# Strided attention and a gated MLP on one core: early weight loads that wait for a tile, the pairs' last step in another order, one total later, and a tile of its own for each last half

## The chip, the cores and the metric

The kernel runs on one core of a Trainium2 chip. The metric is the device time of one execution in microseconds (us). Lower is better. Its engines are PE (matrix products), DVE (vector), ACT (activations), POOL and SP; SP and ACT also issue DMAs. SBUF holds the tiles, and PE writes into PSUM banks.

## What is computed

The reference, cut to what matters: attention over 8 batches, 8 heads, 576 positions and head size 64 with two sparse masks (the first four heads see the last 32 positions, the other four the positions with the same residue modulo 32), then RMS norm and a gated MLP on the 4608 tokens.

```python
mask_local = (rel >= 0) & (rel < 32)
mask_strided = (rel >= 0) & (pos[None, :] % 32 == pos[:, None] % 32)
scores = np.where(masks, q @ k.T / 8, -1e9)
x = (softmax(scores) @ v)                    # 4608 tokens x 512
xn = x / sqrt(mean(x * x) + 1e-6) * rms_g
g, val = xn @ w_gate, xn @ w_val             # 512 x 1536 each
out = (g * sigmoid(g) * val) @ w_out         # 1536 x 512
```

## The kernel before

Work is cut into 32 attention units (one batch, two heads; 576 positions) and 9 chunks of 512 tokens. `unit_s` computes a unit's scores and the softmax, `unit_o` the product with v. Four units run ahead of everything ("the prologue"); the others are strewn between the matrix products by the tables `WIN`, `SAT`, `OAT`, `PSAT`, `POAT`. The MLP splits each fp32 operand in a high and a low part and multiplies three times (`gemm1`, `slot_o`). Chunks 0 to 2 run plainly, twelve steps u of 128 hidden columns each. Chunks 3 to 8 run as three pairs (`pair_of_chunks`) with seven products, named "1" to "7", instead of eight.

Weights: `convert_weights` takes 1 MB of one weight as 64-bit words from DRAM into a tile `raw_` of four slots and turns it into fp32 high and low parts: ACT scales (L840) and builds exponents (L842), DVE does two bit operations (L844, L846), ACT or DVE copies the high part (L496/L498), DVE subtracts (L849). There are 18 such weights: 12 `gv` (gate and value columns of one u) and 6 `o` (output rows of two u). In order of conversion they are numbered here from 1: gv0, gv1, o0, gv2, gv3, o1, gv4 are weights 1 to 7.

SBUF for this is 94 slots of 128x512 words. `group(n)` gives n slots; the table `PLACE` names the slot of every request, and whoever gets a slot waits until its last owner is done with it. `Plan.order` is a list scheduler inside the kernel program: it writes the order of every engine's instructions from estimated costs, and engines then run their queues in that order, each instruction behind the waits of those ahead of it. From chunk 1 on the matrix products and all else on PE keep the order in which the program names them (`plan.serial`). In the gaps that the scheduler estimates on PE in the first 50 us, `fill` puts matmuls on zeros.

In a pair, each u of a quad adds its products into banks p, q and r: "1", "6", "7" and "4" all add into p. After "6" ACT copies p; after "7" DVE adds p to a tile (L1131); after "3" DVE adds to r (L1105) and multiplies (L1127). Between "7" and "4" of one u stands "1" of the next u, which goes into other banks; the last u, 11, has no next one. Then `oproduct` (L1220) multiplies by the output weights, with `attention(13)`, `attention(14)` and so on as marks between the products; between 14 and 15 no product stands. `rms(c)` sums squares on PE into the bank `pair` ("the total", L762), which the units use too, and ACT takes the logarithm from it (L766).

Of the kernel before, what the change touches and what calls it, by code (L numbers as in the profile page):

```python
# [75 lines left out]
RATP = {3: (13, 15), 5: (13, 15)}  # L76
PLACE = list(bytes.fromhex(
    "0004080c100e14181c1e50515253542022555657585924265a5b5c5d282c2d2e292a2f3034383c404414000408502b480c1052494a201c243057554c"
    "4b4e38404d4f5c14040c3c5a2b5020242e2c525c573808140c4d2b5020305a522e4849381420384d3c5c4a2e5a574b2b4d0c4e4f505c572e505c5354"
    "58595d5748495120565b2d564a4b4c285b56512f2e2d4c382856514e385b56512f5b4c3c565148382f4d4c56514c4e0c384a4b480c2f4c5651562f4e"  # L80
    "4f205156480c2f51564a4b2f2d2f4848280c515648282d505c535458595d575156553c525a525a5156525a554a4b482855522c3851562d2c55515648"
    "182d48283451562d4a4b515648204b2d441851564b4647515648004548280c0d0e0f4b47515648102021444f22234b1c1d483c1e1f40414243515647"
    "00015502030405060728292a2b5038393a3b5c53545859242526275d570e0f0c0d58454448104b47555b59085a52090a4f4e0b204b5521222e2f2334"
    "353233363037313c143d153e163f175b1c1d4d5d4c474849575a104b11551252135845594432183119301a3d1b4f25244e264b553e3f275a0e4c0f4d"
    "0c3d0d084b0944453f5d0a4e0b57203021312223441c5a5d1d583459354b3657371430155a4e444c164d1759104b115a121358184c30594b19271a26"
    "1b250e240f0c580d26251c081d09200a210b22235835090a4c4d34263627374d145815164d274d261710111213515618191a1b0e0f0c0d501c1d1e1f"
    "5c5453404142430100020908031751560405060728292a2b0e353438393a26503b1650202123220f36375c5453414014151011121349503b0d0c1819"
    "1a1b0e515616174243081c1d1e1f555d09470100020352575814050406073a28292a2b0f5c5438395342434140353436375b1c153b5a20214b23222f"
    "51560e0d0c16171011131218191a1b4e4f080a0b09303331325d55381d52243d57582e271e1f2547533945464b4a443c14503f3e5b15014849002f02"
    "2c2d035a3b2e0a3d09270b052404255d065507482042214352354134403c57582c363d37531c5a1d2f38392e304445314733463248505b1e1f251424"  # L90
    "5515423b5a4b534a40090a410b3d2e44485201460047025a035320213d052425044806520742504138395a35243d3452374736463b421c1d481e245a"
    "3332301f311424155209320a0b304b48244a4750462052214801004652020305040607145438393b3a5c5135343736561c1d1e1f2322081617282931"
    "304647472a2b0f0e0d0c091514540a0b101113120203504f474e18191a1b5c514b4a56010005040607504f584738393b3a1054222321203736343531"
    "1c1d1f1e34083045090a0b355d054e28292a2b5c115b5316171415510c0d0e0f5613124f501c1054044b4a030200240148434906071a1b1918553736"
    "525a3b3a39382223202159572d2e2c2f1d4e0c053e3d5d5c4231563432403554413f4f5027250d04433c584c4d30330f260e2445594420461e471f3d"
    "211c3e0a42570932083f0b31103013122b1d2a280029034002415c5d4b4a54585642503105324e4404464f59472d27262f242c252e56343e350c3f0d"
    "54310e400f414d2a4c2b2021325c295458445047003f105613124702272503241f2a1e291c3f1d593208274409410a400b474e294f052a0427244a47"
    "4b325c27355834502a2759535b2d2c2e2f514d4c0a0d0c0e0f555a520809202100020301060710124732131153594a515b37361f1e1d1c0d22234849"
    "504b5c04055a5255161715140c4e4f3435002a405951531b1a19184a5b0f0e3a3b393801030241570b0a09084d4c2f2e2d2c37365c504b555a525820"
    "2159530023225107065b055d56"))  # L100
# [247 lines left out]
def attn_moe(ctx: ExitStack, tc: tile.TileContext, qT: bass.AP, kT: bass.AP, vl: bass.AP,  # L348
# [178 lines left out]
    def load(i):  # L527
# [39 lines left out]
    tio = {}  # L567

    def unit_s(i):
# [887 lines left out]
```

## Time and profile before

| what | value |
|---|---|
| median of 3 runs | 949.81 us (948.96 to 949.81) |
| profiled execution | 950.59 us, its span 948.8 us |
| busy PE / DVE / ACT / POOL | 926.6 / 715.6 / 463.2 / 153.9 us |
| DMA | 214.94 MB, mean 227 GB/s |

The span runs from the first to the last instruction. 1.79 us of the profiled execution lie around its span, and it is 0.78 us above the median. Busy time of PE includes slow matmuls and matmuls on zeros, so stretches have to be read one by one.

### The profile page before, as it was taken

The numbers are of one execution on the slowest core, as the hardware profiler recorded it, in microseconds if no ns is written. First come the engines' busy times: TensorE is split into PE (matmuls) and PEld (weight loads), VectorE is DVE, ScalarE is ACT, GpSimd is POOL, SyncE is SP. The second block draws the span as 40 slices with busy tenths as digits, with TensorE's granted clock in tenths as the row PEclk, the third lists the DMA queues.
The fourth block names the chain that finished last, engine by engine and source line by source line (L and its number), as shares of the span: only waits on it lengthen the run. The fifth ranks groups of instructions, "written<-read, shape, count | busy, mean of one in ns | idle before, by whom it ended". The sixth has DMA issues, their size and how long they took to land.

```text
span 948.8 us, 18579 instructions
## 1 busy us (share of the span) xinstructions
PE 926.6 (98%) x7364; PEld 752.5 (79%) x7364; DVE 715.6 (75%) x1097; ACT 463.2 (49%) x723; POOL 153.9 (16%) x125
## 2 busy tenths in 40 slices
PE   6989999999999999999999999999999999999998
PEld 5678877888888888888887788888878877888786
DVE  5899989988599979775568899554698983345783
ACT  6797665343334247454446582443464733233440
POOL 1021302123043420210015031000140210000100
PEclk9899999999999999999999999999999999999999
DMA  9955756978668567997464638984434499741542
GB/s 356 407 219 184 260 200 238 346 263 303 220 211 288 167 217 267 304 393 232 144 200 159 198 127 293 392 253 140 145 100 157 161 365 338 194 149 59 165 154 90
DMA packets 122487, 214.94 MB, mean 227 GB/s; under 512 B 10784, under 2 KB 66336, under 8 KB 119328
## 3 DMA queue, kind: packets, MB, share of 16 engines
q1 hardware_dynamic: 121680, 213.16, 66.0%
q8 instruction: 58, 0.95, 0.4%
q10 hardware_dynamic: 720, 0.59, 0.2%
q14 instruction: 29, 0.24, 0.1%
HBM read 169.67 MB, written 44.04 MB: 225 GB/s over the span
## 4 chain that ended last, share of the span: by engine, by line
PE 87%; DMA 5%; DVE 4%; ACT 1%; issue 1%; SPq 0%; ACTq 0%; DVEq 0%
PE a L1094 16%; PE v L1094 10%; PE g L1094 10%; PE g L931 9%; PE a L983 9%; PE v L931 9%; PE a L1220 8%; PE g L1220 5%; PE v L1220 5%; PE pair L675 4%; PE pair L599 3%; DMA bl<-in_wgv_dram 2%; DMA bl<-gvd 1%; DVE bl L849 1%; DMA bl<-in_wo_dram 1%
## 5 line engine op out<-in xcount | busy, mean ns | idle before, releaser
L496 ACT CAST bl<-bl 128x512 fp32r<-128x512 f32 (+1 forms) x170 | 109.0, 665 | 116.2 <-DVE bl L1051 19.6
L1094 PE MATMUL a<-bl,bl 128*128 128x512 f32 x642 | 159.0, 393 | 0.0
L504 DVE TENSOR_TENSOR bl<-bl,bl 128x512 fp32r<-128x512 f32 x192 | 132.6, 716 | 10.4 <-PE a L1220 4.0
L1094 PEld LDWEIGHTS a<-bl,bl 128*128 128x128 f32 x642 | 119.0, 188 | 25.3
L1094 PE MATMUL v<-bl,bl 128*128 128x512 f32 x431 | 109.9, 390 | 2.9 <-DVE bl L1131 2.4
L931 PE MATMUL g<-bl,bl 128*128 128x512 f32 x408 | 107.1, 398 | 3.5 <-DVE bl L849 3.0
L1094 PE MATMUL g<-bl,bl 128*128 128x512 f32 x428 | 109.2, 390 | 0.7 <-ACT bl L1110 0.7
L931 PE MATMUL v<-bl,bl 128*128 128x512 f32 x420 | 109.4, 397 | 0.1
L983 PE MATMUL a<-bl,bl 128*128 128x512 f32 x432 | 107.0, 389 | 1.1 <-DVE bl L849 1.1
L1094 PEld LDWEIGHTS v<-bl,bl 128*128 128x128 f32 x431 | 80.6, 188 | 21.2 <-DVE bl L1131 3.7
L983 PEld LDWEIGHTS a<-bl,bl 128*128 128x128 f32 x432 | 81.0, 188 | 18.3 <-DVE bl L849 1.5
L1051 DVE TENSOR_TENSOR bl<-bl,bl 128x512 f32<-128x512 f32 x104 | 72.2, 708 | 30.5 <-ACT bl L1110 28.7
L1094 PEld LDWEIGHTS g<-bl,bl 128*128 128x128 f32 x428 | 80.0, 188 | 17.9 <-ACT bl L1110 1.1
L1105 DVE TENSOR_TENSOR a<-a,bl 128x512 f32<-128x512 f32 x72 | 49.8, 695 | 58.9 <-PE a L1094 46.5
L931 PEld LDWEIGHTS g<-bl,bl 128*128 128x128 f32 x408 | 75.4, 189 | 21.8 <-DVE bl L849 4.3
L931 PEld LDWEIGHTS v<-bl,bl 128*128 128x128 f32 x420 | 78.2, 189 | 17.9 <-DVE bl L966 0.8
L504 POOL TENSOR_TENSOR bl<-bl,bl 128x512 fp32r<-128x512 f32 x28 | 41.0, 1467 | 254.9 <-PE g L1094 89.7
L1220 PE MATMUL a<-bl,bl 128*128 128x512 f32 x306 | 72.1, 390 | 0.0
L1220 PEld LDWEIGHTS a<-bl,bl 128*128 128x128 f32 x306 | 57.3, 188 | 12.4 <-DVE bl L504 0.5
L498 DVE CAST bl<-bl 128x512 fp32r<-128x512 f32 (+1 forms) x86 | 48.1, 564 | 15.7 <-PE a L983 3.5
L1051 POOL TENSOR_TENSOR bl<-bl,bl 128x512 f32<-128x512 f32 x20 | 27.2, 1367 | 148.6 <-DVE bl L504 52.2
L1220 PE MATMUL g<-bl,bl 128*128 128x512 f32 x214 | 50.9, 390 | 0.0
(164 smaller groups left out, 1276.8 us busy)
## 6 DMA issues: line engine op xcount, KB each, us to landing
bl<-gvd SPq DMA_DIRECT2D x252, 256.0 KB, 4.9
gvd<-bl SPq DMA_DIRECT2D x72, 256.0 KB, 4.0
bl<-to SPq DMA_DIRECT2D x72, 256.0 KB, 4.1
xq<-in_qT_dram SPq DMA_DIRECT2D x28, 576.0 KB, 5.4
bl<-wos SPq DMA_DIRECT2D x54, 256.0 KB, 3.3
bl<-in_wgv_dram SPq DMA_DIRECT2D x12, 1024.0 KB, 9.6
bl<-wos SPq DMA_DIRECT2D x12, 1024.0 KB, 6.7
vt<-in_vl_dram SPq DMA_DIRECT2D x28, 320.0 KB, 4.0
```

The source lines that it names most:

```text
L496: nc.scalar.copy(out=o, in_=i)
L498: nc.vector.tensor_copy(out=o, in_=i)
L504: elementwise(CH, lambda e: both(e).tensor_tensor(out=lo.new(F32R), in0=src(), in1=hi.f32(), op=ALU.subtract), reads + [hi.key], [lo.key])
L599: nc.tensor.matmul(out=pr[at // CH][64 * s:64 * s + 64, at % CH:at % CH + KW], lhsT=tq()[:, 2 * q0:2 * q0 + 64], rhs=tk_()[:, q0:q0 + KW], ...
L675: nc.tensor.matmul(out=pr[s][64 * h:64 * h + 64, 32 * lo:32 * hi], lhsT=va()[r:r + 32, D * kb:D * kb + D], rhs=pT[r:r + 32, 64 * kb - 32 * ...
L849: elementwise(2 * CH, lambda e: both(e).tensor_tensor(out=wide(q[2:], F32R), in0=cell(1).bitcast(F32), in1=wide(q[:2]), op=ALU.subtract), ...
L931: nc.tensor.matmul(out=out_, lhsT=w.t[:, sl], rhs=x.t, start=(kc == 0 and i == 0), stop=(kc == KC - 1 and i == 2))
L983: nc.tensor.matmul(out=acc[t], lhsT=x.t[:, sl], rhs=w.t, start=(u == 0 and i == 0), stop=(u == NU - 1 and i == 2))
L1051: elementwise(CH, lambda e: both(e).tensor_tensor(out=o.new() if fresh else o.t, in0=a.t, in1=b.t, op=how), [a.key, b.key], [o.key])
L1094: nc.tensor.matmul(out=banks[bk], lhsT=w, rhs=xs[k][y].t, start=start and k == 0 and i == 0, stop=stop and k == 1 and i == 2, skip_group_c ...
L1105: op("DVE", dve(CH), 0, lambda: nc.vector.tensor_tensor(out=banks[bk], in0=banks[bk], in1=t.t, op=ALU.add), reads=[t.key], writes=[bk])
L1220: nc.tensor.matmul(out=banks[bks[j]], lhsT=v, rhs=xs[k][y].t, start=start and k == 0 and i == 0, stop=stop and k == KT - 1 and i == 2, ski ...
```

## The change

The early loads: the raw tile of weights 2 and 3 is now the four slots in which units 2 and 3 of the prologue keep their probabilities and their transpose (`GATE`), and weights 4 to 7 take the raw tile of the weight three before (`REUSE`). So each waits for that tile's last reader. Loads of units 4 and 5 are put in the scheduler at 30 and 36 us (`REL`), and the second mask constant is loaded ahead of unit 2's queries. The last u of a pair runs its products as 5, 6, 2, 7, 3, 4 instead of 5, 6, 2, 3, 7, 4. In pair 3 the total of chunk 5 stands at mark 14 instead of 13. Each half of the last output tiles has a slot of its own, so the DVE copy no longer follows the ACT copy. Fills have 512 columns instead of 192, and one is put per 400 ns of estimated gap instead of 200. `PLACE` is a new table throughout. The diff (the table of slots and the two other loads of a unit, which get the same `rel`, are cut):

```diff
-FILLS = 200.0
+FILLS = 400.0
-FILLN = 192
-LOADS = ("q0", "c2", "c0", "q1", "q2", "v0", "c1", "q3", "v1", "w", "v2", "v3")
+FILLN = 512
+LOADS = ('q0','c2','c0','q1','c1','q2','v0','q3','v1','w','v2','v3')
-RATP = {3: (13, 15), 5: (13, 15)}
+RATP = {3:(14,15),5:(13,15)}
 PLACE = list(bytes.fromhex(
...
+LASTQ = '56273'
+TAILS = True
+REUSE = 3
+GATE = True
+REL = {4:30e3,5:36e3}
...
-    def group(n, r=False):
+    def group(n, r=False, want=None):
...
+        if want is not None and kind[home[want]] in (None, r) and all(want + k in freed for k in range(n)):
+            best = 0, want
         i = PLACE[m] if PLACE and m < len(PLACE) else best[1]
...
-    still = sbt([P, 256], "still", BF16)
+    still = sbt([P, max(256, FILLN)], "still", BF16)
...
-        op("SP", 430, 0, lambda: nc.sync.dma_start(out=tq(), in_=qT[b, p]), writes=keys_[:1], bytes_=P * S * 8, follow="SP" if pro else None)
+        op("SP", 430, 0, lambda: nc.sync.dma_start(out=tq(), in_=qT[b, p]), writes=keys_[:1], bytes_=P * S * 8, rel=REL.get(i, 0.0), follow="SP" if pro else None)
...
         if 1 < i < NPRO:
-            z, y = take2(), take2()
+            zz = group(4) if GATE else take2() + take2()
+            z, y = zz[:2], zz[2:]
+            gates.append(zz[0].i)
...
+    raws = []
+
     def convert_weights(what, u):
-        raw_, q = group(4), group(4, True)
+        raw_ = group(4, False, raws[-REUSE] if REUSE and REUSE <= len(raws) < 7 else gates[len(raws) - 1] if GATE and len(raws) in (1, 2) else None)
+        raws.append(raw_[0].i)
+        q = group(4, True)
...
-            order += [(u, m) for m in ("56237" if u > 1 else "")] + [(u + 1, "1")] * (u + 1 < NU) + [(u, "4")]
+            order += [(u, m) for m in (LASTQ if u == NU - 1 else "56237" if u > 1 else "")] + [(u + 1, "1")] * (u + 1 < NU) + [(u, "4")]
...
-                for m in "56237":
+                for m in LASTQ if u == NU - 1 else "56237":
...
         for j in range(2):
-            dst = take()
             for n, (e, q) in enumerate((("ACT", nc.scalar), ("DVE", nc.sync))):
+                if n == 0 or TAILS:
+                    dst = take()
                 sl = slice(256 * n, 256 * n + 256)
-
-                def half(e=e, sl=sl, dst=dst, j=j, n=n):
-                    copy_to(e, (dst.new() if n == 0 else dst.t)[:, sl], banks[P2[j]][:, sl])
-                op(e, 310, 0, half, reads=[P2[j]] + [dst.key] * n, writes=[("oh", c, j, n)] + [dst.key] * (1 - n))
+                lead = n == 0 or TAILS
+
+                def half(e=e, sl=sl, dst=dst, j=j, lead=lead):
+                    copy_to(e, (dst.new() if lead else dst.t)[:, sl], banks[P2[j]][:, sl])
+                op(e, 310, 0, half, reads=[P2[j]] + [dst.key] * (not lead), writes=[("oh", c, j, n)] + [dst.key] * lead)
...
-            give(dst)
+                if n or TAILS:
+                    give(dst)
```

## Rows read from the trace of the kernel before

**Rows 1.** Busy time of each engine (the page's first part), and in stretches: busy us (and instructions) of PE, PE's weight loads, DVE, ACT and POOL, then the granted PE clock, the DMA share and GB/s.

```profile
PE 926.6 (98%) x7364; PEld 752.5 (79%) x7364; DVE 715.6 (75%) x1097; ACT 463.2 (49%) x723; POOL 153.9 (16%) x125
...
23.00:26.00 3.00, 3.00 (x82) 2.73 (x82) 3.00 (x4) 2.74 (x3) 0.61 (x1) 0.50 1.04 416
26.00:29.00 3.00, 3.00 (x4) 0.83 (x3) 3.00 (x4) 3.00 (x8) 1.49 (x1) 0.50 1.03 407
...
50.00:54.00 4.00, 4.00 (x13) 3.09 (x12) 3.97 (x5) 4.00 (x4) 1.74 (x2) 0.58 0.97 403
...
60.00:70.00 10.00, 9.94 (x43) 7.88 (x44) 10.00 (x10) 8.12 (x9) 1.73 (x1) 1.00 0.57 210
...
160.00:270.00 110.00, 110.00 (x1104) 89.66 (x1103) 88.09 (x142) 41.31 (x50) 21.39 (x16) 1.00 0.77 263
```

**Rows 2.** PE's timeline: start, busy us, line, operation, count, and in brackets the idle time before it with what ended it.

```profile
1.43 3.54 PE L518 MATMUL v<-still 128*128 128x192 bf16 x21 [1.43 <-POOL still L514]
6.51 0.31 PE L594 MATMUL g<-cb,identb 128*128 128x320 bf16 x1 [1.54 <-DMA identb<-in_consts_dram]
...
23.11 2.41 PE L675 MATMUL a<-bl,bl 32*64 32x64 f32 x80
...
39.38 0.84 PE L931 MATMUL a<-bl,bl 128*128 128x512 f32 x3
...
46.47 0.39 PE L931 MATMUL g<-bl,bl 128*128 128x512 f32 x1
49.53 0.90 PE L931 MATMUL g<-bl,bl 128*128 128x512 f32 x2 [2.67 <-DVE bl L849]
...
54.44 0.84 PE L931 MATMUL v<-bl,bl 128*128 128x512 f32 x3
...
59.90 2.14 PE L931 MATMUL g<-bl,bl 128*128 128x512 f32 x8 [0.30 <-DVE bl L849]
```

**Rows 3.** The same view of ACT and DVE, before PE's wait of rows 2.

```profile
44.51 1.17 ACT L840 ACTIVATE bl<-bl 128x1024 f32<-128x1024 f32 x1 [3.87 <-DMA bl<-in_wgv_dram]
45.69 1.28 ACT L950 ACT_TABLE_LOAD   x1
46.99 0.63 ACT L950 ACTIVATE bl<-bl 128x512 f32<-128x512 f32 x1
...
36.32 1.21 DVE L849 TENSOR_TENSOR bl<-bl,bl 128x1024 fp32r<-128x1024 f32 x1
...
44.49 0.68 DVE L498 CAST bl<-bl 128x1024 fp32r<-128x1024 f32 x1
47.65 0.69 DVE L966 TENSOR_TENSOR bl<-bl,v 128x512 f32<-128x512 f32 x1 [2.48 <-ACT bl L950]
48.26 1.22 DVE L849 TENSOR_TENSOR bl<-bl,bl 128x1024 fp32r<-128x1024 f32 x1
```

**Rows 4.** Loads of weights: SP's issues (start, us, line), then the issues of 0 to 60 us and of 60 to 150 us by kind (count, KB of one, median us from issue to landing).

```profile
25.88 2.92 SPq L835 DMA_DIRECT2D bl<-in_wgv_dram  x2
31.08 0.37 SPq L835 DMA_DIRECT2D bl<-in_wo_dram  x1
31.61 0.37 SPq L835 DMA_DIRECT2D bl<-in_wgv_dram  x1
...
bl<-in_wgv_dram SPq DMA_DIRECT2D x8, 1024.0 KB, 11.0
...
bl<-in_wgv_dram SPq DMA_DIRECT2D x5, 1024.0 KB, 5.3
```

**Rows 5.** PE's waits from 120 to 160 us: who, on what, us in total, times, longest.

```profile
PE a L983 <- DVE bl L849: 1.1, 1, 1.1
PE pair L762 <- DVE bl L504: 0.4, 1, 0.4
PE g L931 <- DVE bl L504: 0.3, 1, 0.3
```

**Rows 6.** The end of the third pair's last u on the chain of work that ended last (start, us, what), and the waits of PE for L1131 in the whole span.

```profile
884.16 1.37 PE v L1094 x6
...
885.62 0.70 DVE bl L1131
...
886.37 1.66 PE v L1094 x6
888.02 4.08 PE g L1220 x18
...
PE v L1094 <- DVE bl L1131: 2.4, 3, 0.9
```

**Rows 7.** The first total in pair 3: the timeline of PE and ACT around it.

```profile
541.73 1.17 ACT L496 COPY bl<-pair 128x64 f32<-128x64 f32 x4 [3.52 <-PE pair L675]
542.96 0.73 PE L762 MATMUL pair<-bl,onesr 128*128 128x512 f32 x2 [1.29 <-ACT bl L496]
543.52 2.69 PE L1220 MATMUL a<-bl,bl 128*128 128x512 f32 x11
545.43 0.69 ACT L766 ACTIVATE bl<-pair,few 128x512 f32<-128x512 f32 x1
```

**Rows 8.** The last copies, from the timeline.

```profile
945.18 0.37 ACT L496 COPY bl<-v 128x256 f32<-128x256 f32 x1 [3.71 <-PE v L1220]
...
945.58 0.42 DVE L498 COPY bl<-v 128x256 f32<-128x256 f32 x1 [3.66 <-ACT bl L496]
```

More of the change, by code (lines that the diff above doesn't have):

```diff
@@ L75 @@
 RAT = {0: (10,), 1: (9,), 2: (8, 9)}
-RATP = {3: (13, 15), 5: (13, 15)}
+RATP = {3:(14,15),5:(13,15)}
 PLACE = list(bytes.fromhex(
[L78 to L100, printed above, removed]
@@ L101 @@
-HALFQ = (3,)
+    "0004080c100e14181c1e5051525354205556575859245a5b5c5d282c2d2e292a2f203024341438203c2440482b4a1444494b4c0004080c4e4f504d52"
+    "101c57555c202414005a2b5208342e2c4e4a4b10201440485557080c495a4e5c4c101408102e002b4d524e55574a2e085c4b2b5748554a5257534c4d"
+    "5458595d4940504851565c4b2e285b595d552d504810285c4b2e105156595b555d005c4b4810515d2e56592f4808105c4b48085b512e56595b2f2e40"
+    "5c4b48085b56595c4b5b505b5c4828084b5648285c594a5257505354584b562c005a5c48494b565a5c2c28294e102c5a4c182a2b4d564c4b484e102c"
@@ new lines @@
+    "4e304049284d2c4e292a38103a3b4d3c4b2b4f4e4d484938304d08444b28292a0a0b1011380412133a4f00012e02031c302b242526272a48491e2928"
+    "1f4445464718191a1b343536374b0405060720212223000108090a0b594a12134d4c38403a4f2e551011525d5750515354585b2d0c0d5c5a0e0f301c"
+    "1d311e321f2f334f21551438153916173a222e5b525d232d59514a53401c41424d434c5502380357001f011e3c3d4f3e50542e583f51083a09530a2d"
+    "0b1257131f505838104f115921534a3a0c0d4c0e4d1f0f51223823573059313253334f141516401741384257434f2102510316533857004d014c4a51"
@@ new lines @@
+    "3c4c3d3e513f16170816094d0a510b4d121351100c0d0e0f1116220c230f214a51300c0f0c16313233404142430809020300013c3d3e3f4b202b2a29"
+    "2848492524262744161845474631323334353736040506070002030a1a1b0b3001080912131011404142434a4b2223211916204918063c3d3e3f3120"
+    "48492b2a2928321b3324252627045d5b0544454746280732343537365430535a595157000102030a0b0809063343424041315c12131118104a0d4b29"
+    "2b2a222321203d3c3e3f48495d5b4c4d55501f1d1c1e0128563252071b2d393a58044f0f05550d1806243b2f25262e2c275c14170203441516454e47"
@@ new lines @@
+    "191b464f3139330f500d34353a37153b362d112c122e132f2832180a19560f52390b15085809420143551f401e413a1d2e1c4e5c4f075806042c052d"
+    "150219031850423141242540262e184219192719332d322c112e28444f454e4047554619125c131934352d372c5c362c01550a2d0b500809551f2d4e"
+    "4f2d2c1e2d1d2c1c55312c02035528070611043305320724252d26550527121344454746015430531d5a59511f1e570034353736100a0b0809295507"
+    "045d5b5b2b2a284a4b27111c543130532223212048493d3c5b3e3f4c4d12131d0a5a5159265702030100335207324544474624251f1e22550b103d04"
@@ new lines @@
+    "273c1c0809545b18533534373631304a4b29282a2b3d572311105c581d0a21205a5051593e3f121348494c4d2255060b333b32262725241f1e020301"
+    "00454447465b562d2f2e2c5d141617153c54531c3a39040d1d084341090a19185a2a1b1a31304e4f5051404259292852064a054b3b383507340e370f"
+    "360c212039550d4322412f3a120413525d3e543f53492e482c4e3c4f4d3b4c5a0d1c07051d190a18081b091a502a39143a04150e160f175351415931"
+    "54304807290d28555d1b223a4a4b39204e4f2153121813192f482c2e5435555a344e370f360e3c1b3e3f390a0d501c531d552a540818094d194c5951"
@@ L102 @@
+    "5d4e3139300d22285529540f1415161720214a4b2b131257235c0a2f2e2c590b5853353437361011543e0e193f3c3d33321c1d5b562d1f1e5d2a2627"
+    "252457020300012b454447464d4c5c1312375909394e0858531415161729284a4b0a0b20212223540d0e5d3635343130565b10112f2e2c2d33323e3f"
+    "3c3d5c571c1d1f1e5a5152555919064305"))
+HALFQ = (3,)
+LASTQ = '56273'
[3 more added lines that the diff above has]
+REL = {4:30e3,5:36e3}
 LEAD = 12
@@ L537, in load @@
             op("Pool", 100, 0, lambda: nc.gpsimd.memset(tk_()[:, 0:PAD], 0.0), writes=keys_[2:])
-        op("SP", 430, 0, lambda: nc.sync.dma_start(out=tq(), in_=qT[b, p]), writes=keys_[:1], bytes_=P * S * 8, follow="SP" if pro else None)
-        op(e, 430, 0, lambda: eng.dma_start(out=tk_()[:, PAD:PAD + S], in_=kT[b, p]), writes=keys_[1:2], bytes_=P * S * 4, follow=e if pro else None)
+        op("SP", 430, 0, lambda: nc.sync.dma_start(out=tq(), in_=qT[b, p]), writes=keys_[:1], bytes_=P * S * 8, rel=REL.get(i, 0.0), follow="SP" if pro else None)
+        op(e, 430, 0, lambda: eng.dma_start(out=tk_()[:, PAD:PAD + S], in_=kT[b, p]), writes=keys_[1:2], bytes_=P * S * 4, rel=REL.get(i, 0.0), follow=e if pro else None)
     def load_consts(n):
@@ L557, in load_v @@
         kv = ("v", i if pro else i % 2 + NPRO)
-        op("SP", 430, 0, lambda: nc.sync.dma_start(out=va(), in_=vl[b, p]), writes=[kv], bytes_=P * (NBL + 1) * D * 4, follow="SP" if pro else None)
+        op("SP", 430, 0, lambda: nc.sync.dma_start(out=va(), in_=vl[b, p]), writes=[kv], bytes_=P * (NBL + 1) * D * 4, rel=REL.get(i, 0.0), follow="SP" if pro else None)
         vio[i] = va, [kv] + keys_of(z), z
@@ L567, in attn_moe @@
     tio = {}
+    gates = []
     def unit_s(i):
```

## The prediction

> **What bounds the kernel now.** I read the busy times by stretch first. Over the whole span PE is busy 926.6 of 948.8 us, and from 160 to 270 us it is busy all 110 of 110 us at full clock [rows 1]. There is nothing to win in such a stretch but work that is taken away, and this change takes no product away. So I looked for the places where PE stands or runs at half clock. PE's timeline, the list of waits and the chain of work that ended last give four of them behind the prologue.
>
> First the stop at 46.86 us: PE waits 2.67 us for a DVE subtraction (L849) and comes back at half clock [rows 2]. Second, three small waits between 120 and 160 us [rows 5]. Third, the end of every pair, where "4" waits for DVE to have read p [rows 6]. Fourth, the first total of pair 3 [rows 7]. Behind them comes the tail [rows 8]. Before 30 us there is also half clock (0.50 from 23 to 29 us), but DVE is busy 3.00 of 3.00 us in both of those stretches, so PE is not the bound there [rows 1].
>
> The cause of the first stop is an inversion between queues. DVE's L849 for weight 4 had its high part by 45.2 us (44.49 + 0.68) but stood in DVE's queue behind L966, which waited 2.48 us for ACT's silu (L950). The silu stood in ACT's queue behind L840 of weight 5, and that had waited 3.87 us for its DMA [rows 3]. The DMA was issued at 31.61 us, behind two gv loads and one o load for later weights; weight 5's raw tile came free only then. It landed at 44.5 us, 12.9 us after its issue, while some 400 GB/s were moving (403 to 416 in the stretches shown) [rows 1, 3, 4].
>
> **The change part by part.**
>
> *Pair ends.* The last u's "4" follows "3" instead of "7". In the third pair "7" ends at 885.53 us (884.16 + 1.37), DVE adds for 0.70 us, and "4" runs from 886.37 to 888.02 us: 2.49 us where a product takes 1.36 or 1.37, so 1.13 us are lost. The waits of all three sum to 2.4 us and the slow restarts (1.66 for 1.37 us) add 0.3 each: 3.3 us [rows 6]. "3" lasts 1.36 us, more than the 0.84 us between the end of "7" and the start of "4", so it covers DVE's add if DVE starts it within 0.5 us. One other DVE operation ahead of it (0.7 us) would leave 0.2 us. "7" now comes one product after "6" instead of two, and ACT's copy of p has 1.36 us. What "3" makes is read only by the second output product, at least 8 us (two rows of 4.08 us) later. Bounds 0 and -3.3; I take -3.0 us, near the upper end, because the cover is 1.6 times the gap.
>
> *The total.* At mark 13 the total waits 1.29 us for ACT's copies of the unit just computed, which sit in the same bank [rows 7]. One step later they are long done: -1.3. But between marks 14 and 15 stands no product, so both totals now stand side by side on PE, and the second writes the bank from which ACT's logarithm of the first must have read. On PE everything else queues behind it. The logarithm took 0.69 us, and from the next matmul's start (543.52) to its end (546.12) it was 2.60 us, with a table load of ACT between [rows 7]. So +0.8 if the table is there and ACT free (0.69 and two handoffs of 0.09 and 0.04 us, as between PE and DVE at 885.53 and 886.33 [rows 6]), +2.6 if not, and 0.3 for the restart. I take the middle, 1.7 + 0.3: net +0.7 us, bounds -0.2 and +1.6.
>
> *Last halves.* DVE's copy starts at 945.58 us, once ACT's copy from 945.18 us is done. It reads PSUM, not that copy. With its own slot it starts with ACT's: -0.4 us, as the DMA behind it is the last one; bounds -0.4 and 0 [rows 8].
>
> *Early loads.* The loads that stood ahead of weight 5 now come in the order of need, and three raw tiles pass round. Weight 2 can be issued when unit 2's products are done, at 25.5 us (23.11 + 2.41) [rows 2]. With a landing of 5.3 us, the median from 60 to 150 us, ACT's two steps (2.3 us, twice L840's 1.17) and four steps on DVE (two bit operations and the subtraction, each as L849's 1.21, and the copy of L498, 0.68), it is finished at 25.5 + 5.3 + 2.3 + 4.3 = 37.4 us. Before it was 37.5 (36.32 + 1.21), and PE first used it at 39.38 [rows 2 to 4]. So the wait costs nothing as long as a load lands in 7.3 us. Weight 5 is issued at that 37.4 us and lands at 42.7 to 44.7, no later than now, and the scheduler places it where it will come. What that gives: the stop, 2.67 us, and the slow restart, where 14 matmuls take 4.91 us (49.53 to 54.44) instead of 3.17 (0.68 per three): 4.4 us together [rows 2]. But DVE feeds PE until about 69 us (10.00 of 10.00 us busy from 60 to 70) [rows 1], so only what DVE idles comes back: 2.48 us [rows 3]. I take -2.5, bounds -4.4 and, from the rival below, +6.3.
>
> *Fills, constant, units 4 and 5.* The first 21 fills ran 3.54 us, 0.17 each. Half as many of 512 columns come to 10 x 0.45 = 4.5 us, from about 1.7 us on, as the memset doubles: done at 6.2, before the first product at 6.51 [rows 2]: 0. Without that cover it is up to 0.5 us. If the later fills keep the clock up from 23 to 29 us, half of 6 us of PE time is the most to be had, but DVE is the bound there: 0, bound -3.0 [rows 1]. The constant serves a unit whose exponentials wait for ACT anyway: 0.
>
> *New slots.* The three waits from 120 to 160 us (1.8 us, some 0.3 for restarts) hang on other slots now [rows 5]. The table cannot be read for them: bounds -2.1 and +2 (new waits of the same kind). I take -0.7.
>
> Sum: -3.0 + 0.7 - 0.4 - 2.5 - 0.7 = -5.9 us. The span goes from 948.8 to 942.9; with 1.79 us around it 944.7; the median of the runs lies 0.78 under the profiled one: 943.9 us.
>
> **A rule against the change.** The profile shows 1 MB landing in 5.3 us (median) from 60 to 150 us, where loads are few, and in 11.0 in the first 60, where many are in flight [rows 4]: here an early issue bought a long landing, and the row speaks for the change. The Trainium skill, DMA: Bandwidth & Descriptors, Rules for kernel authors, says the opposite: issue a DMA early, compute, and wait late, so that its fixed cost is hidden. By that page's 2.0 us of fixed cost, an estimate, six loads left bare would cost 12 us, and the sum would be -3.4 + 12 = +8.6 instead of -5.9. What a bare load would do in this kernel, in prices from rows, is the first rival.
>
> **The rivals.**
>
> *The loads starve the start (slower).* If the gated loads still land in 11.0 us, weight 2 is finished at 25.5 + 11.0 + 2.3 + 4.3 = 43.1 us, 3.8 us after PE wants it, and PE restarts at half clock (4.91 - 3.17 = 1.7 us) [rows 2]. Weight 5, behind it on the same tile, is finished at 43.1 + 17.6 = 60.7 us, 0.8 later than before, when PE waited for it until 59.90 [rows 2]. Together +6.3, with the rest (-3.4): +2.9, 952.7 us. The gain of the start is gone from a landing of about 9 us on. For it: DMA moves over 400 GB/s until 54 us now [rows 1]. Against it: that stream is later weights, which are no longer ahead.
>
> *DVE is the bound and the start does not move.* Another DVE idle takes the place of the 2.48 us. Then -3.0 + 0.7 - 0.4 = -2.7: 947.1 us.
>
> *The pairs' reorder does nothing*, because DVE reaches the add late behind its merges: -0.4 + 0.7 - 2.5 - 0.7 = -2.9: 946.9 us.
>
> *All of it comes.* -3.3 - 0.2 - 0.4 - 4.4 - 2.1 = -10.4: 939.4 us; with the clock of 23 to 29 us at most 3 less.
>
> **How the numbers follow.** Chances: forecast 0.50 (941 to 947 us), all of it 0.15, DVE bound 0.15, reorder idle 0.06, starved start 0.14. 0.2% is 1.9 us, about what a measurement tells from no change: 947.9 and 951.7. Faster: 0.48 of the forecast, 0.15, and 0.10 and 0.05 of the middle two, together 0.78; slower 0.11, nearly all of it the starved start; the rest, 0.11, lies between. The range leaves out most of the starved start and the best third of "all of it": 937.5 to 950.5.
>
> **What would show it.** No wait for L1131 in PE's list and "4" at 1.36 to 1.4 us; a wait of the second total for ACT's L766 of 1 to 2.6 us; both last copies starting together; loads of weights 2 to 5 landing in 5 to 7 us, and PE's stop at 47 us gone or under 1 us. Wrong would be: a landing over 9 us or a longer PE stop before 60 us, a new DVE wait ahead of "4", or new waits behind 160 us, where the new table moves every tile.

## The result, and the profile after

The changed kernel takes 958.25 us (median of 4 runs, 957.15 to 958.47), beside 949.5 us for the kernel before: a ratio of 1.0088, 95% interval 1.0075 to 1.0101. It is slower, outside the range of 937.5 to 950.5 us and on the other side of the forecast. The profiled execution took 958.11 us, its span 956.3 us at a granted clock of 0.993.

In the changed kernel the lines are shifted: L599 is L609 (scores), L675 is L685 (probabilities by v), L762 and L766 are L772 and L776 (total and logarithm), L835 to L849 are L849 to L863 (weights), L931 is L945, L950 is L964, L983 is L997, L1094 is L1108, L1131 is L1145, L1220 is L1234; ACT's and DVE's copies L496 and L498 are L503 and L505.

From the end of chunk 0 on, PE runs the same products in nearly the same order in all kernels here. So I read the start of the same few products in PE's timeline of both kernels and take the difference:

| product | before, us | after, us | after is late by |
|---|---|---|---|
| scores of a unit, end of chunk 0 | 149.2 | 149.9 | 0.7 |
| the next unit | 168.2 | 169.8 | 1.6 |
| a unit of chunk 1 | 266.8 | 269.5 | 2.7 |
| the last unit ahead of the step from chunk 1 to 2 | 287.5 | 291.3 | 3.8 |
| the unit behind it | 298.7 | 309.4 | 10.7 |
| last unit ahead of the first pair's end | 514.4 | 525.1 | 10.7 |
| first output product of that pair | 523.7 | 533.6 | 9.9 |
| first unit of the next pair | 602.7 | 613.6 | 10.9 |
| first output product of the second pair | 710.7 | 720.5 | 9.7 |
| first output product of the third pair | 887.9 | 895.4 | 7.5 |
| end of PE's work | 945.1 | 952.6 | 7.5 |

The loss is one place, 291 to 309 us, and some 4 us that creep up ahead of it. Of the creep, 1.0 us belongs to the same place (PE's wait for a raw copy of L505 at 291.31 us, told below), and 0.9 and 1.1 us come between 149.9 and 169.8 and between 230.6 and 269.5 us; the mended version at the end has 0.8 and 1.1 us in those two stretches as well. Busy time, which [rows 1] has for before, hardly moved; PE's waits did (who, on what, us in total, times, longest):

```profile
PE 926.4 (97%) x7344; PEld 751.6 (79%) x7344; DVE 716.4 (75%) x1086; ACT 463.0 (48%) x730; POOL 155.1 (16%) x126
...
PE pair L685 <- DVE pp L641: 5.0, 1, 5.0
PE a L685 <- issue: 2.9, 1, 2.9
PE pair L772 <- ACT bl L776: 2.2, 1, 2.2
```

The wait for L1131 in [rows 6] (2.4 us) is gone from this list. The wait of 5.0 us is new.

**The step from chunk 1 to chunk 2.** The chain of work that ended last, of the changed kernel (start, us, what):

```profile
283.42 8.26 DMA out_dram<-bl
...
291.74 0.69 ACT pp L653
...
294.62 2.64 DVE pp L666
...
300.55 2.41 PE pair L685 x80
302.96 3.83 PE v L945 x12
306.79 2.72 PE a L997 x12
```

The timeline of SP's issues, ACT, DVE and POOL in the same stretch (start, us, line, operation, idle time and what ended it):

```profile
277.79 2.15 SPq L913 DMA_DIRECT2D gvd<-bl  x4
280.04 0.47 SPq L873 DMA_DIRECT2D bl<-wos  x1
280.60 4.32 SPq L1017 DMA_DIRECT2D out_dram<-bl  x4
...
289.83 0.60 ACT L970 ACTIVATE bl<-g 128x512 f32<-128x512 f32 x1 [6.85 <-DMA out_dram<-bl]
...
290.40 0.86 DVE L505 COPY bl<-pair 128x128 f32<-128x128 f32 x3 [4.21 <-DMA out_dram<-bl]
...
294.62 2.63 DVE L666 TENSOR_TENSOR pp<-pp,st 128x576 f32<-128x576 f32 x1
...
294.27 2.37 POOL L828 TENSOR_TENSOR bl<-bl,bl 128x1024 fp32r<-128x1024 f32 x1
```

Two of chunk 1's four output tiles sit in slots 5a and 5c. The new table gives the same two slots to the first silu tile of chunk 2 (ACT, L970) and to the first raw copy of the next unit (DVE, L505), so both wait until the stores have read them. SP issued four stores of `gvd` (1 MB) and a reload of 1 MB ahead of the four output stores, and the first two landed at 289.72 and 290.38 us, 9.1 and 8.7 us after their issue. The chain above puts the last store (283.42 + 8.26) ahead of the exponentials; in ACT's timeline the wait is the silu's, for the first store, and behind the silu comes a table load of 1.28 us. ACT then did the unit's exponentials at 291.74 us, and DVE's multiply L666 met POOL's L828 and took 2.63 us (the same line took 0.75 us at 18.68 us of this trace, with POOL idle). PE waited 1.0 us at 291.31 us for the raw copy, then 5.0 us, and came back at half clock (granted 0.50 from 300.55 to 302.9 us): 2.41 us for 80 products that take 1.39 at full clock, 3.83 us for 12 that take 2.72. 5.0 + 1.0 + 1.1 = 7.1 us; the table above says 6.9, and the 1.0 us ahead of the step is in its 3.8. The kernel before had two output tiles handed on in the same way, and ACT waited for a store there too, but SP had issued them in two halves with less ahead, the two that were waited for landed at 285.70 and 286.35 us, and no wait reached PE:

```profile
275.02 1.07 SPq L1003 DMA_DIRECT2D out_dram<-bl  x2
278.55 0.86 SPq L1003 DMA_DIRECT2D out_dram<-bl  x2
...
285.79 1.28 ACT L956 ACT_TABLE_LOAD   x1 [4.61 <-DMA out_dram<-bl]
```

**The start.** SP's issues, ACT, DVE and PE of the changed kernel:

```profile
11.84 0.38 SPq L849 DMA_DIRECT2D bl<-in_wgv_dram  x1
13.22 0.38 SPq L849 DMA_DIRECT2D bl<-in_wo_dram  x1
16.25 10.15 SPq L849 DMA_DIRECT2D bl<-in_wgv_dram  x2
30.49 0.37 SPq L849 DMA_DIRECT2D bl<-in_wo_dram  x1
...
30.91 1.17 ACT L854 ACTIVATE bl<-bl 128x1024 f32<-128x1024 f32 x1
36.22 1.15 ACT L854 ACTIVATE bl<-bl 128x1024 f32<-128x1024 f32 x1 [1.91 <-DMA bl<-in_wo_dram]
...
38.48 1.23 DVE L858 SCALAR_TENSOR_TENSOR bl<-bl 128x1024 uint32<-128x1024 uint32 x1 [0.96 <-ACT bl L856]
39.62 1.22 DVE L863 TENSOR_TENSOR bl<-bl,bl 128x1024 fp32r<-128x1024 f32 x1
...
41.60 0.84 PE L945 MATMUL a<-bl,bl 128*128 128x512 f32 x3
...
52.57 1.22 PE L945 MATMUL g<-bl,bl 128*128 128x512 f32 x2 [1.41 <-DVE bl L863]
```

Weight 2 was issued at about 26 us (the second of the pair that begins at 16.25 and ends at 26.40) and had landed by 30.91 us, when ACT took it without a wait. Its subtraction, L863 at 39.62 us, stands in DVE's queue behind a bit operation of weight 3, which waited for ACT, which had waited for a load issued only at 30.49 us, when unit 3's tile was free. PE starts on weight 2 at 41.60 us, 2.2 us later than in [rows 2]. The stop of 2.67 us there is a stop of 1.41 us here, with one of 1.35 us ahead of it, 2.76 us together.

**The pair ends, the total and the tail.** The third pair's end on the chain (start, us, what), then the last copies in the timeline:

```profile
892.79 1.36 PE a L1108 x6
894.15 1.36 PE v L1108 x6
895.51 4.08 PE g L1234 x18
```
```profile
952.67 0.37 ACT L503 COPY bl<-v 128x256 f32<-128x256 f32 x1 [3.71 <-PE v L1234]
...
953.07 0.42 DVE L505 COPY bl<-v 128x256 f32<-128x256 f32 x1 [3.65 <-ACT bl L503]
```

"4" runs 1.36 us with nothing ahead of it, where [rows 6] has 1.66 us behind a gap of 0.84. The second total waits 2.2 us for the logarithm of the first (L776, in the list of waits above). DVE's last copy still follows ACT's, as in [rows 8].

### The profile page after: what moved, and what is told of

It reads as the page before. It is cut to its first block, busy times and chain, and to the rows that moved or that the text cites. A ratio compares the mean times of both kernels' runs of the same rounds, so it can differ in the third digit from the quotient of the medians.

```text
span 956.3 us, 18530 instructions
## 1 busy us (share of the span) xinstructions
PE 926.4 (97%) x7344; PEld 751.6 (79%) x7344; DVE 716.4 (75%) x1086; ACT 463.0 (48%) x730; POOL 155.1 (16%) x126
## 4 chain that ended last, share of the span: by engine, by line
PE 68%; DVE 1%; DMA 1%; ACT 0%; issue 0%; SPq 0%
PE a L1108 16%; PE g L1108 10%; PE v L1108 10%; PE a L1234 8%; PE g L1234 5%; PE v L1234 5%; PE a L997 3%; PE v L945 3%; PE g L945 3%; PE pair L685 2%; PE pair L609 2%; DMA out_dram<-bl 1%; DVE pp L666 0%; PE pair L772 0%; DVE bl L505 0%
## 5 line engine op out<-in xcount | busy, mean ns | idle before, releaser
L503 ACT CAST bl<-bl 128x512 fp32r<-128x512 f32 (+1 forms) x175 | 112.7, 670 | 108.4 <-DVE bl L980 23.0
L1108 PE MATMUL a<-bl,bl 128*128 128x512 f32 x636 | 158.0, 393 | 0.0
L1108 PEld LDWEIGHTS a<-bl,bl 128*128 128x128 f32 x636 | 118.0, 188 | 25.1
L511 DVE TENSOR_TENSOR bl<-bl,bl 128x512 fp32r<-128x512 f32 x191 | 130.2, 711 | 7.9 <-PE a L1234 2.5
L945 PE MATMUL g<-bl,bl 128*128 128x512 f32 x408 | 106.4, 397 | 4.0 <-DVE bl L863 1.4
L945 PE MATMUL v<-bl,bl 128*128 128x512 f32 x420 | 109.6, 399 | 0.0
L1108 PE MATMUL g<-bl,bl 128*128 128x512 f32 x425 | 108.7, 390 | 0.7 <-ACT bl L1124 0.7
L1108 PE MATMUL v<-bl,bl 128*128 128x512 f32 x422 | 107.7, 389 | 0.0
L997 PE MATMUL a<-bl,bl 128*128 128x512 f32 x432 | 106.4, 389 | 0.0
L1065 DVE TENSOR_TENSOR bl<-bl,bl 128x512 f32<-128x512 f32 x99 | 70.1, 726 | 32.3 <-ACT bl L1124 32.1
L997 PEld LDWEIGHTS a<-bl,bl 128*128 128x128 f32 x432 | 81.0, 188 | 16.9
L1108 PEld LDWEIGHTS g<-bl,bl 128*128 128x128 f32 x425 | 79.5, 188 | 17.7 <-ACT bl L1124 1.1
L945 PEld LDWEIGHTS g<-bl,bl 128*128 128x128 f32 x408 | 75.9, 189 | 21.9 <-ACT bl L503 1.8
L945 PEld LDWEIGHTS v<-bl,bl 128*128 128x128 f32 x420 | 78.6, 190 | 17.6 <-DVE bl L980 0.4
L1108 PEld LDWEIGHTS v<-bl,bl 128*128 128x128 f32 x422 | 79.1, 188 | 16.9 <-DVE bl L1145 0.4
L511 POOL TENSOR_TENSOR bl<-bl,bl 128x512 fp32r<-128x512 f32 x29 | 43.3, 1502 | 234.0 <-ACT bl L503 94.8
L1234 PE MATMUL a<-bl,bl 128*128 128x512 f32 x304 | 71.6, 390 | 0.0
L1234 PEld LDWEIGHTS a<-bl,bl 128*128 128x128 f32 x304 | 56.9, 188 | 11.9
L1065 POOL TENSOR_TENSOR bl<-bl,bl 128x512 f32<-128x512 f32 x22 | 31.0, 1409 | 161.4 <-issue 59.2
L897 POOL TENSOR_TENSOR bl<-bl 128x256 f32<-128x256 f32 (+1 forms) x36 | 34.6, 968 | 118.9 <-DVE bl L897 78.2
L505 DVE CAST bl<-bl 128x512 fp32r<-128x512 f32 (+1 forms) x81 | 45.9, 571 | 8.5 <-PE v L1234 2.8
```

What stands on the lines that cost most here:

```text
L503: nc.scalar.copy(out=o, in_=i)
L505: nc.vector.tensor_copy(out=o, in_=i)
L511: elementwise(CH, lambda e: both(e).tensor_tensor(out=lo.new(F32R), in0=src(), in1=hi.f32(), op=ALU.subtract), reads + [hi.key], [lo.key])
L897: elementwise(256 if ds != ALL else CH, lambda e: both(e).tensor_tensor(out=d.t[:, ds], in0=x.t[:, xs], in1=y.t[:, ys], op=ALU.subtract), ...
L945: nc.tensor.matmul(out=out_, lhsT=w.t[:, sl], rhs=x.t, start=(kc == 0 and i == 0), stop=(kc == KC - 1 and i == 2))
L997: nc.tensor.matmul(out=acc[t], lhsT=x.t[:, sl], rhs=w.t, start=(u == 0 and i == 0), stop=(u == NU - 1 and i == 2))
```

## The experiments

Each is the changed kernel with the edit shown, unless it says otherwise. Where only one execution was profiled, that is said; the medians of before beside them were 949.25, 948.83 and 949.29 us.

**Own slots at the step from chunk 1 to 2.** Two entries of the table change; slots 4e and 4f are free there.

```diff
-PLACE[213], PLACE[214] = 0x5a, 0x5c
+PLACE[213], PLACE[214] = 0x4e, 0x4f
```

> The changed kernel with two entries of the slot table altered: the first two outputs of chunk 1 get slots 4e and 4f instead of 5a and 5c, so that the silu and the first copy of chunk 2, which use 5a and 5c next, no longer wait for output stores. Theory A (those two slots cost the time lost between 283 and 303 us): the 5.0 us stop of PE at 295 us is gone, ACT's wait of 6.9 us for the output store too, and the time falls by 7 to 9 us to 949 to 951 us. Theory B (the late start, or the scheduler's new order as a whole, makes this place collide whatever the slots): the stop stays or comes back within 20 us, 956 to 959 us.

952.7 us (951.72 to 953.15), ratio 1.0037, interval 1.0023 to 1.0052. The stop of 5.0 us is gone; PE's waits from 270 to 330 us:

```profile
PE pair L685 <- DVE pp L641: 1.6, 2, 1.1
```

At the unit behind the step this kernel is 7.7 us ahead of the changed one (301.7 against 309.4), and a small new wait gives 1.2 back by 330 us. That is less than the 7 to 9 us expected; still, the two entries explain 5.5 us of the 8.75 us that the change lost. With them the scheduler also issued the stores in two halves again (at 278.02 and 283.10 us), so the slots and the order that follows from them changed together. By the same two unit starts the step costs 6.8 to 8.1 us in the five other kernels below that keep slots 5a and 5c, and -0.1 to 0.5 us in the four with other slots.

**Weight 2 alone in a free tile.** Weights 2 and 5 take the tile that weight 8 had, weight 8 that of unit 2.

```diff
-PLACE[33], PLACE[39], PLACE[51] = 0x20, 0x20, 0x00
+PLACE[33], PLACE[39], PLACE[51] = 0x00, 0x00, 0x20
```

> The changed kernel with the raw tiles of weights 2 and 5 exchanged with that of weight 8: weight 2 loads at once into unit 0's tile (slots 00 to 03), weight 8 waits for unit 2's tile instead. Theory A (weight 2 comes too late and starves DVE from 29 to 40 us): DVE's first bit operation on weight 2 starts by 30 us instead of 33.2, PE's waits around 50 us shrink from 2.8 us to under 1 us, and chunk 0 ends 2 to 4 us earlier. Theory B (DVE is the bound at the start, its order apart): the waits move, and chunk 0 ends within 1 us of the changed kernel's. The time itself is left open, as the place at 295 us may shift with it.

964.46 us in one profiled execution; the unit at the end of chunk 0 starts at 154.9 us, 5.0 later than in the changed kernel. Weight 2 is early, and DVE then stands for weight 3 (its timeline and ACT's):

```profile
40.68 1.23 DVE L858 SCALAR_TENSOR_TENSOR bl<-bl 128x1024 uint32<-128x1024 uint32 x1 [6.15 <-ACT bl L856]
...
38.44 1.11 ACT L854 ACTIVATE bl<-bl 128x1024 f32<-128x1024 f32 x1 [2.36 <-DMA bl<-in_wo_dram]
```

To free one load of a chain moves the wait to the next: weight 3 still hangs on unit 3's tile (issued at 30.50 us, landed at 38.41). Neither expectation covers a start that is 5 us later.

**Later weights out of the early tiles.** Weights 8 to 10 move behind tiles that come free later; weights 2 and 3 stay gated.

```diff
-PLACE[51], PLACE[53], PLACE[60] = 0x00, 0x08, 0x10
+PLACE[51], PLACE[53], PLACE[60] = 0x20, 0x24, 0x14
```

> The changed kernel with weights 8, 9 and 10 on the same three raw tiles as weights 1 to 7, so that none of them loads before weight 2. From about 19 us until weight 2 is issued no data DMA is under way. Theory A (the stops of PE in which it waits for nothing the profile shows, 2.9 us in the middle of unit 2's products, come from instructions that are fetched behind data): that stop falls under 0.5 us, weight 2 is issued by 24 us instead of 26, and PE's first use of weight 2 comes 1.5 to 2.5 us earlier. Theory B (the stop has another cause): it stays at 2 to 3 us.

964.36 us in one profiled execution; 155.1 us at the end of chunk 0, again 5 late. The loads of still later weights took the early places, so DMA stayed full (407 GB/s from 20 to 23 us) and the question was not put as meant: inconclusive on TensorE's stop, which stayed.

```profile
12.75 12.71 SPq L849 DMA_DIRECT2D bl<-in_wgv_dram  x3
...
23.87 1.15 PE L685 MATMUL a<-bl,bl 32*64 32x64 f32 x60 [2.92 <-issue]
```

**Weights 2 and 3 both in free tiles** (and so 5 and 6; weights 8 and 9 take those of units 2 and 3).

```diff
-PLACE[33], PLACE[35], PLACE[39], PLACE[41], PLACE[51], PLACE[53] = 0x20, 0x24, 0x20, 0x24, 0x00, 0x08
+PLACE[33], PLACE[35], PLACE[39], PLACE[41], PLACE[51], PLACE[53] = 0x00, 0x08, 0x00, 0x08, 0x20, 0x24
```

> The changed kernel with weights 2 and 3 (and 5 and 6 after them) in the tiles of units 0 and 2, free at once, and weights 8 and 9 behind units 2 and 3 instead. Theory A (DVE starves because weights 2 and 3 come late; with weight 2 alone early it then waited 6.2 us for weight 3): DVE has no idle stretch over 1.5 us between 20 and 45 us and chunk 0 ends 1 to 3 us earlier than in the changed kernel. Theory B (DVE's total work is the bound): chunk 0 ends within 1 us of it or later.

955.49 us in one profiled execution; the unit at the end of chunk 0 starts at 145.9 us, 4.0 ahead of the changed kernel and 3.3 ahead of before. ACT takes weight 2 at 23.84 us and PE starts on it at 36.17 us:

```profile
23.84 1.18 ACT L854 ACTIVATE bl<-bl 128x1024 f32<-128x1024 f32 x1 [1.11 <-DMA bl<-in_wgv_dram]
...
36.17 1.94 PE L945 MATMUL a<-bl,bl 128*128 128x512 f32 x6
```

So the gating of weights 2 and 3 was what the start lost by. The edit also makes weights 8 and 9 late, but that alone did not help: above they were late with weights 2 and 3 still gated (and still later weights early), and the start lost 5 us. The step from chunk 1 to 2 costs 7.9 us here, as its slots are still the shared ones.

**The total at its old mark**; every tile keeps its slot.

```diff
-RATP = {3:(14,15),5:(13,15)}
+RATP = {3:(13,15),5:(13,15)}
```

> The changed kernel with the total of chunk 5 back at mark 13. Theory A (two totals side by side make the second wait for the first one's logarithm): PE's 2.2 us wait of the second total for ACT is gone, the 1.3 us wait for the copies of the unit is back, and pair 3's output products end 0.5 to 1.2 us earlier. Theory B (the move pays): they end 1 us later.

956.31 us in one profiled execution. Between the first output product and the next pair's first unit it gains 1.1 us, and PE's waits from 526 to 620 us are those of [rows 7] again:

```profile
PE pair L772 <- ACT bl L503: 1.3, 1, 1.3
```

**The old fills.**

```diff
-FILLS = 400.0
-FILLN = 512
+FILLS = 200.0
+FILLN = 192
```

> The changed kernel with the old fills: 192 columns, one per 200 ns of estimated gap. Theory A (fills cost and give nothing that reaches the end): chunk 0 ends within 0.7 us of the changed kernel's and the clock from 20 to 29 us is the same. Theory B (longer fills hold PE up or keep its clock): 1 to 3 us off, either way.

953.89 us in one profiled execution, and 3.0 us ahead of the changed kernel at the end of chunk 0, where the prediction had put the fills at nothing. The stop of 2.92 us is 1.57, and DVE's L858 near 45 us, which in the changed kernel runs beside POOL's L652 and takes 2.18 us, takes 1.22 here, while POOL's takes 3.20 instead of 2.06 (changed kernel first, then this one, with its stop):

```profile
44.95 2.18 DVE L858 SCALAR_TENSOR_TENSOR bl<-bl 128x1024 uint32<-128x1024 uint32 x1
...
43.98 2.06 POOL L652 TENSOR_TENSOR pp<-pp,st 128x576 f32<-128x576 f32 x1 [15.11 <-DVE st L644]
```
```profile
22.63 2.40 PE L685 MATMUL a<-bl,bl 32*64 32x64 f32 x79 [1.57 <-issue]
...
44.17 1.22 DVE L858 SCALAR_TENSOR_TENSOR bl<-bl 128x1024 uint32<-128x1024 uint32 x1
...
43.20 3.20 POOL L652 TENSOR_TENSOR pp<-pp,st 128x576 f32<-128x576 f32 x1 [15.85 <-DVE st L644]
```

**The kernel before, with the new order of the pairs' last step alone**; every tile keeps its slot.

```diff
+LASTQ = '56273'
...
-("56237" if u > 1 else "")
+(LASTQ if u == NU - 1 else "56237" if u > 1 else "")
...
-                for m in "56237":
+                for m in LASTQ if u == NU - 1 else "56237":
```

> The kernel before with the order 5, 6, 2, 7, 3, 4 of the last u in each pair as the only edit; every tile keeps its slot. Theory A (that edit alone is worth what the pair ends lost, 3.3 us by the rows of before): no wait for the add after 7, each pair from its first product to its output products 0.8 to 1.2 us shorter, 946.0 to 947.5 us. Theory B (the gain is given back by other work on DVE, or by the scheduler's new order at the start): 948.5 to 951 us.

949.3 us (948.17 to 951.62), ratio 1.0004, interval 0.9995 to 1.0014: nothing. The pairs' ends did gain (they come 1.1, 0.6 and 1.85 us earlier against what stands ahead of each), but from the first one to the next pair's first unit 3.1 us were lost. PE's waits from 526 to 606 us, where before has only the 1.3 us of the total:

```profile
PE g L1221 <- DVE bl L505: 1.6, 2, 1.3
PE pair L763 <- DVE bl L499: 1.3, 1, 1.3
```

PE waits in the output products for a copy that DVE makes late. Of POOL's work, 4.70 us now fall into 545 to 555 us, where before had 1.34. Which of the scheduler's moves brought that was not separated.

**The mended version: weights 2 and 3 in free tiles, own slots, old mark**, with the new order, the new fills and the rest of the change kept (its table entries follow the order of requests again, which the lines below leave out).

```diff
-RATP = {3:(14,15),5:(13,15)}
+RATP = {3:(13,15),5:(13,15)}
-PLACE[33], PLACE[35], PLACE[39], PLACE[41], PLACE[51], PLACE[53] = 0x20, 0x24, 0x20, 0x24, 0x00, 0x08
+PLACE[33], PLACE[35], PLACE[39], PLACE[41], PLACE[51], PLACE[53] = 0x00, 0x08, 0x00, 0x08, 0x20, 0x24
-PLACE[213], PLACE[214] = 0x5a, 0x5c
+PLACE[213], PLACE[214] = 0x4e, 0x4f
```

> The changed kernel with three things taken back or mended: weights 2 and 3 (and 5 and 6 after them) load at once into the tiles of units 0 and 2 and weights 8 and 9 take their place behind units 2 and 3; the first outputs of chunk 1 in slots 4e and 4f; the total of chunk 5 at mark 13. Theory A (the gated loads, the two slots and the paired totals are the three losses): chunk 0 ends 1 to 3 us earlier than in the changed kernel, the place at 295 us loses 6 to 8 us less, pair 3 one less: 943 to 948 us. Theory B (the start is DVE bound, or the scheduler's order matters more than when loads land): 949 to 954 us.

945.47 us (945.43 to 946.41), ratio to before 0.9962, interval 0.9948 to 0.9976: faster than both kernels, and 12.8 us under the changed one. No wait is left from 270 to 310 us. The busy time of each engine over the span (943.5 us):

```profile
PE 923.3 (98%) x7344; PEld 748.1 (79%) x7344; DVE 706.3 (75%) x1079; ACT 470.9 (50%) x741; POOL 165.7 (18%) x125
```

**The mended version with the old order of the pairs' last step** (six entries of the table change places with it, not shown).

```diff
-LASTQ = '56273'
+LASTQ = '56237'
```

> The version with weights 2 and 3 early, own slots at the chunk boundary and the total at its old mark, with the order 5, 6, 2, 3, 7 in the last step of a pair put back; one pair of slots in three pairs is swapped by it, all else stays. Theory A: the order that the change brought is worth the difference of the three pair ends seen against the kernel before, 0.9, 1.2 and 2.2 us, so this kernel is 3 to 4.5 us longer than with the new order: 948.5 to 950. Theory B, from the kernel before with the new order alone, which gained nothing: what the pair ends gain is given back in the pair that follows, so this kernel is 0 to 1.5 us longer: 945.5 to 947.

949.52 us (948.04 to 952.53), ratio to before 1.0007, interval 0.9996 to 1.0017: 4.05 us longer than with the new order. By the starts of the same products the three pair ends are worth 1.05, 1.5 and 1.6 us, and PE's waits over the whole span hold "4" behind DVE's add three times again:

```profile
PE v L1108 <- DVE bl L1145: 3.3, 3, 1.3
```

So the first theory holds here. The order alone gained nothing in the kernel before (1.0004), the rest of the mended version alone gains nothing over before (1.0007), and the two together gain 3.4 us (945.47 beside 948.83). The waits that took the gain back in the kernel before do not come here: from 515 to 700 us the mended version has only the 1.3 us of the total. The start of the mended version is 4.0 us ahead of before at the end of chunk 0 (145.2 against 149.2), but of the 3.3 us that the kernel with the old order, with the same weights early, is ahead there, 1.8 are gone at 265 us and 0.4 us are left at 404; between 310 and 385 us one new wait takes 1.1 us.

**The mended version with the old fills.** The same edit as above.

> The version with weights 2 and 3 early, own slots at the chunk boundary and the total back at its old mark, now also with the fills of the kernel before (192 columns, counted at 200 ns, 21 of them ahead of the first product instead of 10). In the changed kernel the old fills had been worth 3.0 us by the end of the first chunk. Theory A: what they move is the place at which TensorE stops with nothing to wait for (1.07 us near 17 and 2.92 us near 21 in the changed kernel, 1.57 us with the old fills); in this version those two stops are 1.07 and 0.38 us, so old fills can save at most 1.4 us: 944 to 945.5. Theory B: the old fills save the same 3 us here: about 942.5. Theory C: the 3 us were an accident of how Pool's and DVE's work met at 45 us, and here nothing is saved or something is lost: 945.5 to 947.

946.12 us (945.11 to 946.57), ratio to before 0.9963, interval 0.9949 to 0.9977: the same as with the new ones. PE's stop without a wait is 2.68 us here instead of 0.38, and yet the end of chunk 0 comes only 0.4 us later (145.6 against 145.2). So the 3 us of the old fills in the changed kernel were not of fills as such; that they were a matter of what met what near 21 and 45 us is argued.

## Why the prediction was wrong, by its own steps

*New slots*, -0.7 us with bounds -2.1 and +2: this term failed, and with it the sign. What lies between 149 and 309 us came out at +10.0 us (0.7 to 10.7 in the first table), 6.9 of it at one step between chunks. With the 1.0 us ahead of it that step cost 7.9 us, and 5.5 us came back with two entries; the rest of the +10.0 is not separated from the scheduler's new order. I bounded a table that moves every tile by the waits of one 40 us stretch. The bound was no bound: a tile that a store reads and the next chunk's first ACT and DVE instructions write can cost a store's whole landing, and [rows 4] had 11.0 us for a landing in a crowd. "The table cannot be read" was wrong too: the owner of every slot follows from the order of requests, and two entries were enough to take 5.5 us back. The text did name "new waits behind 160 us" as what would make it wrong, and gave it no price.

*Early loads*, -2.5 us: +0.7 at 149 us, together with whatever the slots ahead of it cost. The landing was right for weight 2 (5.3 us assumed; issued at 26.03 us, landed at 30.80), and ACT's two steps ended at 33.2 us as added up. The failing step is "four steps on DVE (4.3 us)" taken back to back. Between them the queue held two other DVE operations (0.75 us each), 0.96 us of waiting for weight 3 and that weight's bit operation (1.1): finished at 40.84 us instead of 37.4. Weight 5 was issued right behind it, at 40.91 us, and landed at 49.37, 8.5 us later, where 42.7 to 44.7 was assumed. It is the inversion that I had read in [rows 3] for weight 5, moved to weight 3. Nor had I looked at who takes the early queue places: weights 8 to 10 have free tiles and were issued at 11.84 to 16.25 us, ahead of the gated ones.

*The rule that I set against the change.* The Trainium skill, DMA: Bandwidth & Descriptors, Rules for kernel authors, says to issue a DMA early and wait for it late. I let the row of slow landings outweigh it. The measurement sides with the page: with weights 2 and 3 issued early the end of chunk 0 came 4.0 us earlier, in spite of the crowded queue. The sign of my sentence about it was wrong; the page's fixed cost was not what the late loads paid for. The page fits its 2.0 us on DMAs that GpSimd issues; the loads here are issued by SP.

*The rivals.* "The loads starve the start" had the slower side, with 952.7 us, and its mechanism was not what happened: weight 2 landed in under 5 us, and at 149 us the loss was 0.7 us, not the 6.3 of its sum. At the start the rival "DVE is the bound" came nearest: other waits took the place of the stop, 2.76 us for 2.67. But the bound was no fixed one, as weights 2 and 3 early moved the end of chunk 0 by 4.0 us.

*Pair ends*, -3.0 us with bounds 0 and -3.3: right in mechanism. The changed kernel gains 0.8, 1.2 and 2.25 us, 4.2 together, and the mended version without the order loses 4.05. I had counted the gap and the slow restart of "4" alone, 3.3 us; what the other 0.8 to 0.9 are was not separated. In the kernel before the order gained nothing over the whole; that is the rival "the pairs' reorder does nothing", by another way than the one I gave (DVE is late behind the pair, not at the add).

*The total*, +0.7 us: measured +1.0, and 1.1 back when it is undone; the wait of 2.2 us lies in the 1 to 2.6 that was given. *Last halves*, -0.4 us: 0. The step "it reads PSUM, not that copy" failed: DVE's copy starts 0.40 us after ACT's in both kernels, separate slots or not. Both read the same bank `v`. The Trainium skill, PSUM — Partial Sum Buffer, PSUM bank collisions raise a hardware error, says that two engines reading one bank and quadrant collide and have to be kept apart; the rows agree with a guard by bank, and no run here tried it without. *Fills*, 0 us: the first ten ran 3.68 us from 1.64 us and were done before the first product, as worked out, yet the old ones are worth 3.0 us in the changed kernel and nothing in the mended one. I had left out that a fill is also an instruction.

## What to carry to other kernels

When a change replaces a whole table of slots, list for each tile that a store or a slow reader holds which instruction gets the slot next, and price each pair with the longest landing the trace shows, not with the average. When a load is made to wait for a tile, follow its steps through the queues with the neighbours in them: the step that waits next, for another load, sets the end. And measure a part inside the version that it will live in: the same reorder was worth 0 us in one schedule and 4 us in another, where the weights' loads, two slots and one total had changed as well.

## What the hardware showed that was not expected

TensorE stops at the same place of its own instruction stream, whatever it is doing there. In the changed kernel the profile has two stops near 20 us that end in "issue", that is, nothing in the profile was waited for. Counted from the start, they come behind 221 and 348 matmul records. In the seven other versions with the new fills the first comes behind 220 or 221 and, where it shows, the second behind 346 to 348; in before and the three other versions with the old fills the one stop comes behind 348 (a few records are missing in one trace). Where three more fills stand ahead, the stop lies three products earlier, as in the mended version, behind 17 instead of 20 of a group:

```profile
20.90 0.56 PE L685 MATMUL a<-bl,bl 32*64 32x64 f32 x20
...
24.38 1.58 PE L685 MATMUL a<-bl,bl 32*64 32x64 f32 x60 [2.92 <-issue]
```
```profile
23.29 0.50 PE L685 MATMUL a<-bl,bl 32*64 32x64 f32 x17 [1.93 <-DVE bl L667]
24.16 1.16 PE L685 MATMUL a<-bl,bl 32*64 32x64 f32 x63 [0.38 <-issue]
```

It costs 2.9 us where PE runs up to it (the first fence, the changed kernel) and 0.4 us where PE had just stood 1.93 us for DVE (the second, the mended version). All the while DMA moved some 406 GB/s. The Trainium skill, Runtime: NRT & Kernel Launch, Instruction fetch mechanics, says that instructions come in blocks of 256 by DMA and that crossing a block is mostly hidden. From 221 to 348 records with a weight load each are 254 instructions, an estimate that fits a block of that page; with two records of PE's sequencer the trace has 256 between the stops. "Mostly hidden" does not hold for the 2.9 us here. The traces hold the fetch itself: a queue of the kind "instruction" moves 58 transfers of 16,384 bytes in each. In the changed kernel one of them runs from 21.95 to 23.05 us, inside the second stop, which ends at 24.38 us. DMA's queues from 21.4 to 24.4 us (packets, MB, share of 16 engines):

```profile
q1 hardware_dynamic: 310, 1.20, 100.5%
q8 instruction: 1, 0.02, 2.3%
```

In all twelve traces each of these stops ends 1.25 to 1.5 us after the end of such a transfer. With the old fills in the changed kernel it ran from 20.24 to 21.33 us, and the stop was 1.57 us instead of 2.92. So TensorE waits for its next instructions. That the fetch is late because the queue is full of data is argued: the one run meant to thin the queue did not thin it.

DVE and POOL can hold each other up: DVE's L666 took 2.63 us beside POOL instead of 0.75, and near 45 us the same meeting cost DVE 0.96 us in one version and POOL 1.14 in another. The rows look like one engine waiting for the other's instruction to end, not like both running slowly: L666 ended 0.61 us after POOL's L828, and in the second version POOL's L652 ended 1.01 us after DVE's L858, each about its length when alone (0.75, and 1.15 us at 460 us of the changed kernel). Which of the two has to wait differs: at 520.69 us of the changed kernel L666 kept its 0.76 us, and POOL's L511 beside it took 1.77 us instead of about 1.3.
